# A two-branch transformer block on one core: the products of ones ahead of the work read a bf16 constant, twelve of them instead of ten

## The chip, the core and the metric

The kernel runs on one core of a Trainium2 chip. A core has five engines that run side by side, each with its own instructions in a fixed order: TensorE (PE) for matrix products, VectorE (DVE), ScalarE (ACT) and GpSimd (POOL) for elementwise work and reductions, and SyncE (SP), which here only issues transfers. PE reads from SBUF and writes to PSUM, which has eight banks; DVE and ACT copy results back. Sixteen DMA engines move data between the chip's memory and SBUF, and within SBUF. Engines wait for one another through semaphores.

The metric is the device time of one execution in microseconds (us). Lower is better.

## What is computed

The input x is 2048 tokens of 448 numbers. It is normalised per token, and two branches read the result. Branch A is linear attention with 16 heads of 28 features, where queries and keys go through a learned map and two softmaxes. Branch B is a dense layer to 1792 with the Mish activation, and one back. The output is x plus both.

```
xn = (x - mean) / sqrt(var + eps)
q, k, v = split(xn @ wqkv)                      # 16 heads of 28
phi(t) = concat(softmax(t @ w_phi), softmax(-t @ w_phi))
kv, z = phi(k)^T @ v, sum over tokens of phi(k)
A = (phi(q) @ kv) / (phi(q) . z + 1e-6), heads joined, @ wo
h = xn @ w1 + b1;  B = (h * tanh(softplus(h))) @ w2
out = x + A + B
```

All inputs and the output are bf16.

## The kernel before

**Tiling.** The 2048 tokens are 16 tiles of 128, taken in 8 pairs numbered u = 0 to 7; pair 7 is tiles 14 and 15. For each pair the kernel takes the statistics of its two tiles (`ln_stats`, L458), normalises them (`ln_pair`, L492 on DVE or L487 on POOL) and transposes them. Pairs 3 and 2 are transposed on PE (L500) and copied out of PSUM by ACT and DVE (L505, L507). The other pairs are transposed by a transfer that SP issues (L512). The transposed pair, in `xnT`, then feeds the products for v, k and q (helper `pair_part`, L430).

**Weights.** The map w_phi is folded into the query and key weights on the chip, so that one product gives the mapped keys. For the keys, the raw weights `WkR` are loaded (L278), turned on PE against an identity matrix (`w_tr`, L548), copied to SBUF in the buffer `Eq` (L505 on ACT and, for half of the second part, L507 on DVE), multiplied on PE by a block-diagonal arrangement of w_phi (`w_mm`, L571) and copied out again (`Wpk`, L505 on ACT). For the queries, the load itself transposes (L287), and one DVE copy (L291) fills in the last columns.

**Later stages.** The products of keys and values are summed over all pairs (L638). The first dense layer runs in 28 pieces (L430 again, with Mish on ACT at L689). The attention output per tile (L712 and the DVE lines 727 to 738) is transposed, and the two output products (L813 and L829) meet in PSUM, where DVE adds x (L778) before the store.

**Order.** The text `ORDER` (from L147) lists all steps by name, and each engine gets its instructions in that order. A step's name tells its kind, pair and engine: `st15d` is the statistics of tile 15 on DVE, `xn7d` the normalising of pair 7 on DVE, `xt7m` its transposing transfer, `lx4s` the load of x for tiles 8 to 11 from SP. A class `Program` works out the semaphores: an instruction waits for those that wrote what it reads, and an engine runs strictly in order. An instruction that waits so holds back all that stand behind it on its engine. This is so for SP too, where the loads and the transposing transfers share one queue.

On PE the order in front is: `z10`, `wtk0a`, `wtk1b` (the turning of the key weights in two halves), `xt3b`, `xt2d` (the transposes of pairs 3 and 2), `wmk1a`, `wmk0a` (the folding for the keys), then `v3F` and the other value, key and query products. On DVE it is: statistics of tiles 7, 4 and 5, normalising of pairs 3 and 2, the copies for `wtk1b`, `xt3b` and `xt2d`, statistics of tiles 15, 14 and 13, `xn7d`, and `qd` (L291). On SP, `xt7m` comes after the first loads, and `lx4s` comes behind it.

**The step that is changed.** `z10` calls `warm(10)` (L370 to L378). It takes one PSUM bank and runs ten products of a 128 x 128 block of ones with a 128 x 512 block of ones. Both are one column of a constant read over and over. Nobody reads the result. The step waits for nothing and stands first on PE.

Of the kernel before, what the change touches and what calls it, by code (L numbers as in the profile page):

```python
# [9 lines left out]
BF16 = mybir.dt.bfloat16  # L10
# [6 lines left out]
P = 128  # L17
# [13 lines left out]
def ap_on(src, dims):  # L31
    return bass.AP(tensor=src.tensor, offset=src.offset, ap=[list(src.ap[0])] + [list(d) for d in dims])
# [112 lines left out]


ORDER = """  # L147
lx3s st7d lx2s lks pi pp lpa table st4d st5d pw z10 st6a rs3a pm rs2t xn3d lvts bd wtk0a pv lvms lx6s xn2d wtk1b xt3b
xt2d wmk1a lqT0 st15d lx0s lqT3 lqT1 lqT2 wmk0a st14d v3Fd rs7a st13d xn7d v2Hd v3Ha k3H k2H lx1s pk k2F v2Fa qd wmq1a
st12d st3d st2d k3F wmq0d lbs xt7m v7Fd lx4s k7F l1ts rs1p rs6a xn1d q2H st10d xn6p l1m2s k7H xt1m st1d st11d v7Hd q3H  # L150
xt6m q3F rs5p xn5p st0d st8d q2F e6 v1Fa st9d q1F xt5m k1H v1Hd rs4t q1H e7 k6H xn4d kn2.1 kn2.0 k1F k6F rs0a e2 v5Fd
# [17 lines left out]
def _kernel(es, nc, A_x, A_wqkv, A_w_phi, A_wo, B_w1, B_b1, B_w2, out):  # L169
    def sb(name, shape, dtype):  # L170
        return es.enter_context(nc.sbuf_tensor(name, shape, dtype))
# [4 lines left out]
    ident = sb("ident", [P, P], BF16)  # L176
# [71 lines left out]
    def bank(b, n=1):  # L248
        return PS[:, b * TCW:(b + n) * TCW]
# [10 lines left out]
    def pb(b):  # L260
        return ("ps", b)
# [107 lines left out]

    def warm(n):  # L370
        b = take1()
        one = nc.const_aps.scalar_like(1.0, ident[:, 0:1])

        def f(e):
            for _ in range(n):
                ins = e.matmul(bank(b)[:, :], ap_on(one, [[0, P]]), ap_on(one, [[0, TCW]]), start=True, stop=True)  # L376
            return ins
        pe(f, [], [pb(b)], f"warm{n}")  # L378
# [25 lines left out]
    def take1():  # L404
        b = min((b for b in range(8) if b - b % 2 not in held), key=lambda b: used[b])
        touch(b)
        return b

    def pe(fn, r, w, tag):
        return op("PE", fn, r=r, w=w, tag=tag)  # L410
# [499 lines left out]
    for n in (4, 8, 10, 12, 14):  # L910
        add(f"z{n}", warm, n)
# [53 lines left out]
```

## Time and profile before

| | before |
|---|---|
| time, median of three runs | 162.64 us (162.0 to 162.92) |
| the profiled execution: time | 161.87 us |
| its span, first to last instruction | 160.0 us |
| PE busy | 154.5 us, 97% of the span |
| DVE, ACT, POOL busy | 64%, 45%, 25% |
| products of ones (L376) | 20 records, 0.84 us to 12.18 us |

The page of the profile has numbered parts. Part 1 gives each engine's busy time. Part 2 cuts the span into 40 slices of 4 us and gives the busy share of each in tenths. Part 4 is the chain of work that ended last, followed back from the last instruction. In rows with an engine, the first number is the start and the second the length, both in us from the span's start; xN counts the instructions that a row merges, and a bracket at the end gives the idle time of the engine ahead of it and what ended it. "PEld" is the loading of a product's stationary operand, "SPq" a transfer being issued on SP's queue. The ends of PE's products are modelled by the profiler, and they overlap: their spacing is read from their starts.

### The profile page before, as it was taken

How to read it: one execution, taken by the hardware profiler on the slowest of the kernel's cores; microseconds unless marked ns; L12 is line 12 of the kernel's file. 1: busy time of each engine (PE TensorE's matmuls, PEld its weight loads, DVE VectorE, ACT ScalarE, POOL GpSimd, SP SyncE). 2: the span in 40 equal slices, each digit the busy share in tenths (PEclk: the TensorE clock that was granted, in tenths of full speed). 3: DMA queues.
4: the chain of work that ended last, by engine and by line, in shares of the span. 5: the costliest groups of instructions: out<-in, count | busy, mean ns of one | idle time of the engine just before them, and what ended most of it. 6: DMA issues, size and time to landing. Idle time of an engine off the chain costs nothing.

```text
span 160.0 us, 2916 instructions
## 1 busy us (share of the span) xinstructions
PE 154.5 (97%) x1193; PEld 75.6 (47%) x1193; DVE 101.6 (64%) x225; ACT 71.9 (45%) x94; POOL 39.5 (25%) x55
## 2 busy tenths in 40 slices
PE   7999989999989999999999999999999999999993
PEld 3447443444434346543444444555545555445552
DVE  0906958699959990307574856959979899311241
ACT  3607897899689984353885685500000000000000
POOL 6700026439998999000000000000000000000000
PEclk9999999999999999999999999999999999999999
DMA  5991489899998299599005300050022212510005
GB/s 142 299 193 48 36 212 217 159 166 172 226 198 201 41 190 353 153 185 83 0 4 105 64 12 4 0 104 16 0 57 49 82 46 57 161 44 0 0 0 201
DMA packets 40058, 17.12 MB, mean 107 GB/s; under 512 B 33965, under 2 KB 39277, under 8 KB 40045
## 3 DMA queue, kind: packets, MB, share of 16 engines
q1 hardware_dynamic: 39436, 16.81, 48.8%
q8 instruction: 9, 0.15, 0.4%
q10 hardware_dynamic: 608, 0.12, 0.4%
q14 instruction: 5, 0.03, 0.1%
HBM read 6.97 MB, written 1.84 MB: 55 GB/s over the span
## 4 chain that ended last, share of the span: by engine, by line
PE 79%; DMA 8%; ACT 6%; DVE 2%; SPq 2%; issue 1%; ACTq 0%; DVEq 0%
PE PS L430 33%; PE PS L813 26%; PE PS L376 7%; PE PS L829 7%; DMA EqT<-actT 3%; DMA xnT<-xn 3%; DMA x_all<-in_A_x_dram 3%; PE PS L712 2%; PE PS L638 2%; ACT actT L670 1%; ACT Wpk L505 1%; ACT actT L609 1%; ACT Eq L505 1%; DVE KVT L650 1%; SPq L678 1%
## 5 line engine op out<-in xcount | busy, mean ns | idle before, releaser
L430 PE MATMUL PS<-xnT,W 128*128 128x512 bf16 (+1 forms) x224 | 45.7, 379 | 0.2 <-ACT actT L689 0.2
L813 PE MATMUL PS<-W,actT 128*128 128x448 bf16 (+1 forms) x224 | 43.3, 351 | 0.0
L689 ACT ACTIVATE actT<-PS,b1T 128x1024 bf16<-128x1024 f32 x28 | 30.1, 1113 | 17.5 <-PE PS L430 13.1
L813 PEld LDWEIGHTS PS<-W,actT 128*128 128x128 bf16 x224 | 21.8, 98 | 20.2 <-issue 0.2
L430 PEld LDWEIGHTS PS<-xnT,W 128*128 128x128 bf16 (+1 forms) x224 | 17.5, 97 | 24.2 <-issue 4.1
L621 POOL TENSOR_TENSOR actT<-actT,rSk 128x896 bf16<-128x896 bf16 x16 | 26.6, 1696 | 5.3 <-DVE rSk L619 5.2
L778 DVE TENSOR_TENSOR x_all<-PS,x_all 128x448 bf16<-128x448 f32 (+1 forms) x16 | 9.2, 614 | 15.2 <-PE PS L829 8.0
L617 DVE TENSOR_REDUCE Sk<-actT 128x32 f32<-128x896 bf16 x16 | 16.6, 1039 | 0.0
L727 DVE COPY Sq<-PS 128x16 f32<-128x16 f32 x32 | 4.0, 168 | 17.1 <-PE PS L712 17.1
L609 ACT ACTIVATE actT<-PS 128x896 bf16<-128x896 f32 x16 | 13.8, 939 | 1.7 <-PE PS L430 1.7
L430 PE MATMUL PS<-Wv,xnT 128*128 128x448 bf16 (+1 forms) x64 | 13.0, 352 | 1.0 <-DMA xnT<-xn 0.6
L430 PE MATMUL PS<-Wpk,xnT 128*128 128x448 bf16 (+1 forms) x64 | 12.8, 353 | 0.2 <-DMA xnT<-xn 0.2
L430 PE MATMUL PS<-Wpq,xnT 128*128 128x448 bf16 (+1 forms) x64 | 12.6, 353 | 0.1
L376 PE MATMUL PS<-const-float32-1.0 128*128 128x512 f32 x20 | 11.3, 732 | 0.8 <-PEq L950 0.8
L458 DVE BATCH_NORM_STATS2 stats<-x_all 128x6 f32<-128x448 bf16 x15 | 9.1, 607 | 4.2 <-DMA x_all<-in_A_x_dram 4.1
L735 DVE TENSOR_TENSOR v_all<-v_all 128x464 f32<-128x464 f32 x16 | 10.3, 643 | 0.6
L731 DVE TENSOR_TENSOR v_all<-PS,Sq 128x464 f32<-128x464 f32 x16 | 10.3, 641 | 0.5
L738 DVE TENSOR_TENSOR xn<-v_all,rden 128x448 bf16<-128x448 f32 x16 | 10.0, 625 | 0.6
L733 DVE TENSOR_TENSOR v_all<-PS,Sq 128x464 f32<-128x464 f32 x16 | 10.1, 630 | 0.0
L670 ACT ACTIVATE actT<-PS 128x896 bf16<-128x896 f32 x10 | 8.7, 922 | 2.4 <-PE PS L430 1.7
L430 PEld LDWEIGHTS PS<-Wv,xnT 128*128 128x128 bf16 (+1 forms) x64 | 5.1, 96 | 6.9 <-issue 1.7
L430 PEld LDWEIGHTS PS<-Wpq,xnT 128*128 128x128 bf16 (+1 forms) x64 | 5.1, 97 | 6.2 <-issue 1.4
(85 smaller groups left out, 117.2 us busy)
## 6 DMA issues: line engine op xcount, KB each, us to landing
W<-in_B_w_dram SPq DMA_DIRECT2D x1, 1568.0 KB, 7.7
out_dram<-x_all SPq DMA_DIRECT2D x7, 224.0 KB, 2.2
W<-in_B_w_dram SPq DMA_DIRECT2D x3, 448.0 KB, 4.6
x_all<-in_A_x_dram SPq DMA_DIRECT2D x4, 224.0 KB, 3.2
x_all<-in_A_x_dram SPq DMA_DIRECT2D x2, 448.0 KB, 4.9
Wo<-in_A_wo_dram SPq DMA_DIRECT2D x2, 336.0 KB, 9.0
W<-in_B_w_dram SPq DMA_DIRECT2D x2, 224.0 KB, 4.9
WkR<-in_A_wqkv_dram SPq DMA_DIRECT2D x1, 392.0 KB, 4.7
```

Source lines behind the costliest of these rows:

```text
L376: ins = e.matmul(bank(b)[:, :], ap_on(one, [[0, P]]), ap_on(one, [[0, TCW]]), start=True, stop=True)
L430: ins = e.matmul(o, lhs(c, k), rhs(c, k), start=first and c in (0, 3), stop=not first and c in (2, 3))
L609: op("ACT", lambda e, s=s: e.activation(E_of(u)[:, s, :, :], two(b, D), ACT.Exp, scale=1.0 if s == 0 else -1.0), r=[pb(b), pb(b + 1)], w=[ ...
L617: op("DVE", lambda e: e.tensor_reduce(Sk[u][:, s, :], Eh(), AX.X, ALU.add), r=[("E", u, s)], w=[("Sk", u, s)], tag=f"Sk{u}.{s}")
L621: op("POOL", lambda e: e.tensor_tensor(Eh(), Eh(), ap_on(rSk[u][:, s, 0:1], [[1, 2 * H], [0, DH]]), ALU.mult), r=[("E", u, s), ("rSk", u, ...
L670: op("ACT", lambda e, s=s: e.activation(Eq_of(u)[:, :, s, :].rearrange("p i (h n) -> p i h n", n=64)[:, :, :, 0:QP], two(b, D).rearrange(" ...
L689: op("ACT", lambda e: e.activation(actT[:, fc, q * 1024:(q + 1) * 1024], bank(b, 2), ACT.Mish, bias=b1T[:, fc:fc + 1]), r=[("b1T",), pb(b) ...
L731: op("DVE", lambda e: e.tensor_tensor(tv(t1[i]), num(0), sx(1), ALU.mult), r=[pb(b), pb(b + 1), ("Sq", i, 1)], w=[("t1", i)], tag=f"ta{t}")
L733: op("DVE", lambda e: e.tensor_tensor(tv(t2), num(1), sx(0), ALU.mult), r=[pb(b), pb(b + 1), ("Sq", i, 0)], w=[("t2",)], tag=f"tb{t}")
L735: op("DVE", lambda e: e.tensor_tensor(t1[i], t1[i], t2, ALU.add), r=[("t1", i), ("t2",)], w=[("t1", i)], tag=f"tc{t}")
L813: ins = e.matmul(bank(b)[:, 0:width(t)], actT[:, fc, tok(t)], W2[:, fc, 0:width(t)], start=first and fc == 0, stop=last and fc == FC - 1)
L829: ins = e.matmul(bank(b)[:, 0:n], oT_of(u)[lo:hi, cc * P:(cc + 1) * P], Wo[lo:hi, cc, 0:n], start=first and c in (0, 3), stop=last and c i ...
```

## The change

The step `z10` in the order becomes `z12`, and the constant that the products read becomes the bf16 one in place of the fp32 one. Nothing else differs. Both constants are written by POOL in the preamble of either kernel.

```
 ORDER = """
-lx3s st7d lx2s lks pi pp lpa table st4d st5d pw z10 st6a rs3a pm rs2t xn3d lvts bd wtk0a pv lvms lx6s xn2d wtk1b xt3b
+lx3s st7d lx2s lks pi pp lpa table st4d st5d pw z12 st6a rs3a pm rs2t xn3d lvts bd wtk0a pv lvms lx6s xn2d wtk1b xt3b
...
     def warm(n):
         b = take1()
-        one = nc.const_aps.scalar_like(1.0, ident[:, 0:1])
+        one = nc.const_aps.tensor(1.0, (P, 1), BF16)

         def f(e):
             for _ in range(n):
```

More of the change, by code (lines that the diff above doesn't have):

```diff
@@ L147 @@
 ORDER = """
-lx3s st7d lx2s lks pi pp lpa table st4d st5d pw z10 st6a rs3a pm rs2t xn3d lvts bd wtk0a pv lvms lx6s xn2d wtk1b xt3b
+lx3s st7d lx2s lks pi pp lpa table st4d st5d pw z12 st6a rs3a pm rs2t xn3d lvts bd wtk0a pv lvms lx6s xn2d wtk1b xt3b
 xt2d wmk1a lqT0 st15d lx0s lqT3 lqT1 lqT2 wmk0a st14d v3Fd rs7a st13d xn7d v2Hd v3Ha k3H k2H lx1s pk k2F v2Fa qd wmq1a
@@ L371, in warm @@
         b = take1()
-        one = nc.const_aps.scalar_like(1.0, ident[:, 0:1])
+        one = nc.const_aps.tensor(1.0, (P, 1), BF16)
         def f(e):
```

## The prediction

> **What bounds the kernel now.** I read the page's parts 1 and 2 first. They say which engine is busy, and when.
>
> ```profile
> span 160.0 us, 2916 instructions
> PE 154.5 (97%) x1193; PEld 75.6 (47%) x1193; DVE 101.6 (64%) x225; ACT 71.9 (45%) x94; POOL 39.5 (25%) x55
> PE   7999989999989999999999999999999999999993
> DVE  0906958699959990307574856959979899311241
> ACT  3607897899689984353885685500000000000000
> POOL 6700026439998999000000000000000000000000
> PEclk9999999999999999999999999999999999999999
> DMA  5991489899998299599005300050022212510005
> ```
>
> PE is busy for 97% of the span. But in slice 2 (8 to 12 us) DVE, ACT and POOL all stand still, and in slices 3 and 4 (12 to 20 us) the DMA engines are mostly idle, while PE is "busy". Something that PE does in front holds the others. The chain that ended last, read from its start, names it:
>
> ```profile
> 0.84 11.34 PE PS L376 x20
> 12.18 0.51 PE PS L548 x10
> ...
> 17.43 0.58 DVE xn L492 x2
> ...
> 19.35 4.34 DMA x_all<-in_A_x_dram
> 23.69 4.47 DMA xnT<-xn
> ...
> 28.29 15.69 PE PS L430 x90
> ```
>
> The products of ones (L376) hold PE to 12.18. Only then come the turned key weights (L548), their copy (ACT), the folded weights, the normalised pair 7 (DVE L492), its transposing transfer on SP's queue, and behind that in the same queue the load of x that feeds PE at 28.29. From there the chain is nearly all PE to the end. So 11.3 us of dummy work lie on the path that sets the end.
>
> **What the ones cost, before and after.** The timeline of PE, asked in short windows, gives the spacing. A row has the start, the length from the first start to the last end, and the count.
>
> ```profile
> 1.82 1.06 PE L376 MATMUL PS<-const-float32-1.0 128*128 128x512 f32 x1
> 1.82 1.91 PE L376 MATMUL PS<-const-float32-1.0 128*128 128x512 f32 x2
> 5.98 1.02 PE L376 MATMUL PS<-const-float32-1.0 128*128 128x512 f32 x2
> 12.02 1.17 PE L548 MATMUL PS<-ident,WkR 112*112 112x112 bf16 x20
> 52.62 0.81 PE L430 MATMUL PS<-xnT,W 128*128 128x512 bf16 x3
> 52.62 1.24 PE L430 MATMUL PS<-xnT,W 128*128 128x512 bf16 x5
> ```
>
> Ten fp32 products leave 20 records (the chain's x20), two each. The first starts at 0.84 and the second at 1.82; from there a further record lengthens the row by 1.91 - 1.06 = 0.85 us. If that spacing held, 14 more from 5.98 would end far behind 12.02, where L548 follows. They are spaced (12.02 - 5.98) / 14 = 0.43 us, half of it. So PE runs at half speed until shortly before 5.98 and at full speed after. The PEclk row shows 9 throughout and does not see it, so I read speed from spacing alone. The sum fits: starts at 0.84, then 1.82 and four more at 0.85 make six records up to about 5.98, and 14 x 0.43 lead from there to 12.02.
>
> A bf16 product of 512 columns is one record; two of them take 1.24 - 0.81 = 0.43 us, so 0.215 us each at full speed, half of an fp32 record. At half speed no row shows one. Its ends are 0.215 (no slower than at full speed) and 0.85 (an fp32 record at half speed). I take 0.43: the ratio of two between the record kinds, applied to 0.85. Then twelve take 12 x 0.43 = 5.2 us and PE is free at 0.84 + 5.2 = 6.0, not at 12.02. At the low end it is free at 3.4. At the high end there are again six slow records to 5.98, then six at 0.43: free at 8.6. [...]
>
> Removed are 20 records of 11.2 us, added 12 of 5.2 us. The constant costs nothing new, since POOL already writes a bf16 one in the preamble, ahead of the first product:
>
> ```profile
> 0.38 0.10 POOL L950 MEMSET const-bfloat16-1.0<- 128x1 bf16 x1
> ```
>
> Nothing else is moved: on DVE, ACT, POOL and SP the same instructions stand in the same order, and the ones keep the first PSUM bank.
>
> **What is late next.** L548 needs the raw key weights. The rows of SP's queue and of the landings (last number: us from issue to landing):
>
> ```profile
> 1.72 0.42 SPq L278 DMA_DIRECT2D WkR<-in_A_wqkv_dram  x1
> WkR<-in_A_wqkv_dram SPq DMA_DIRECT2D x1, 392.0 KB, 4.7
> 4.05 0.49 SPq L268 DMA_DIRECT2D x_all<-in_A_x_dram  x1
> x_all<-in_A_x_dram SPq DMA_DIRECT2D x1, 448.0 KB, 5.3
> 6.46 3.72 SPq L287 DMA_TRANSPOSE WqT<-in_A_wqkv_dram  x3
> WqT<-in_A_wqkv_dram SPq DMA_TRANSPOSE x2, 3.6
> 10.85 0.47 SPq L302 DMA_DIRECT2D b_rows<-in_B_b_dram  x1
> 18.04 1.26 SPq L512 DMA_TRANSPOSE xnT<-xn  x1
> ```
>
> WkR lands at 1.72 + 4.7 = 6.4. PE could therefore start L548 at 6.4 to 6.5, which is 5.5 us earlier, with about 0.4 us of idle time ahead. It makes no difference whether the ones end at 3.4 or at 6.0. These loads wait for nothing that PE does, so they land when they did. Now DVE:
>
> ```profile
> 6.18 1.96 DVE L492 TENSOR_SCALAR xn<-x_all,mv,rstd 128x448 bf16<-128x448 bf16 x6
> 13.31 0.69 DVE L507 CAST Eq<-PS 112x512 bf16<-112x512 f32 x1 [5.17 <-PE PS L548]
> 14.78 0.62 DVE L458 BATCH_NORM_STATS2 stats<-x_all 128x6 f32<-128x448 bf16 x1
> 17.93 0.22 DVE L291 COPY WqT<-WqT 128x256 bf16<-128x256 bf16 x1
> ```
>
> DVE is busy with pairs 3 and 2 until 8.14. L548's 20 products (1.17 us) end by 7.7, so DVE's copy starts at 8.14 to 8.2 instead of 13.31: 5.1 us earlier (its wait of 5.17 for L548 is gone). This is the tightest link, and it sets the sum. Shifted by 5.1, the next steps meet their loads just in time. The statistics of tile 15 come at 9.7, and its x (issued at 4.05) lands at 9.35. WqT is copied at 12.8, and its last transfer (issued near 8.9, 3.6 us) lands at 12.5. The transposing transfer of pair 7 comes at 12.9, and SP's queue is free from 11.3; before, it stood there until 18.04. The load of x behind it moves from 19.35 to 14.2, and the chain quoted above follows it as a block. The DMA engines, idle between 13 and 18, are then busy again from 12.9.
>
> Behind 28.3 I cost the change at nothing. The stages show why the shift should last:
>
> ```profile
> 12.00:15.10 3.10, 2.74 (x51) 2.54 (x50) 1.79 (x4) 2.05 (x4) 0.00 (x0) 1.00 0.17 62
> 15.10:28.30 13.20, 12.18 (x86) 5.88 (x83) 10.68 (x31) 11.43 (x19) 3.57 (x7) 1.00 0.71 145
> 28.30:75.00 46.70, 46.11 (x374) 21.52 (x375) 31.50 (x58) 34.09 (x44) 30.39 (x24) 1.00 0.91 181
> 75.00:160.00 85.00, 82.27 (x671) 40.91 (x669) 53.46 (x123) 20.11 (x19) 0.00 (x0) 1.00 0.19 47
> ```
>
> (Columns: length, busy time of PE, PE loads, DVE, ACT, POOL, then clock, DMA share, GB/s.) PE works 46.1 of 46.7 and 82.3 of 85.0 us, on inputs that all hang on the shifted chain. **The sum**: of the 6.0 us that the ones give back, WkR's landing takes 0.4 and DVE's pairs 3 and 2 another 0.5; what is left is the 5.1 us of DVE's copy. The profiled execution took 161.87 us (1.87 outside the span) and would take 156.8. The median of the three runs stands 0.77 above it, so 162.64 - 5.1 = 157.5.
>
> **The rivals.**
>
> *Half speed lasts one stretch longer.* PE needed some 5.0 us of unbroken work to reach full speed (0.84 to shortly before 5.98). The twelve ones last 5.2, then come some 0.4 us without work. If the rise misses this stretch, PE must earn it again from 6.45, to about 11.5. The 20, 14 and 16 small products ahead of the first value product took 15.14 - 12.02 = 3.1 us at full speed with 2.7 busy; doubled they end near 11.7, a shift of 3.4 instead of 5.1. That gives 159.2. If it misses that stretch too, another 5 us at half speed cost 2.5 more, less the idle 1.4 us of the first two stages above: 160.3. For it: there is nearly no margin. Against it: at half speed the small products leave PE hardly idle, and whatever counts PE's work sees a gap of only 0.4. [...] Chance 0.18.
>
> *It is slower: PE stays at half speed through the front.* Place: 6.45 to 24 us, where the work is broken up. Price: a stretch of T us at half speed loses T/2 of work. The gain of 5.1 plus 1.4 us of idle time is used up at T = 13, that is if the rise comes only at about 19 us. At 24 us it costs 17.5/2 - 1.4 = 7.4, so 2.3 more than is won: 164.9. For it: nothing in the trace shows how soon the speed rises when PE's work is broken up, as it is there. Against it: between 12.0 and 28.3 PE is idle for only 1.4 us of 16.3, and at half speed it would be idle for less. Chance 0.08.
>
> *The transfers are the bound and move no earlier.* DMA share is 0.91 from 28.3 to 75. If this stage can't end sooner, the time is 162 to 163. Against it: its first transfer waits for pair 7 alone, and the engines stand idle ahead of it. Chance 0.06, of which 0.05 is within 0.5%.
>
> *A bf16 record costs as much as an fp32 one*, so the change does only half of what it says. PE is free at 8.6, L548's 1.17 us end at 9.8, DVE copies at 10.0, a shift of 3.3: 159.3. The rows at 52.62 speak against it. Chance 0.02.
>
> **How the numbers follow.** The forecast has 0.66, the rivals 0.18, 0.08, 0.06 and 0.02. Half a per cent of this kernel, 0.8 us, is about what a measurement can tell from no change. Faster by more than that: 0.66 + 0.18 + 0.02 + 0.01 = 0.87. Within it 0.05, slower 0.08. The likeliest time is 157.5. Its own range is 156.5 to 158.4: a run 0.9 us to either side, about the spread of the runs shown (162.0 to 162.92). To reach 8 in 10 the range takes in the half-speed case, up to 160.6.
>
> **What would show it.** In the changed profile: 12 bf16 records of L376, spaced 0.43 us, the last ending near 6.2; L548 first at 6.4 to 6.5; DVE's copy (L507) at 8.2 with less than 0.3 us of idle time ahead instead of 5.17; the first transposing transfer of xn at 12.9 instead of 18.04; the 90 products of the chain at 23.2 instead of 28.29; a span near 155. The spacing of the 448-column products in front shows the speed. If it is 0.37 us rather than half of that, the half-speed rivals hold, and the time at which it halves says which. The prediction is wrong if L548 starts early and the transfer of pair 7 does not, or if both are early and the products near 28 us are not.

## The result and the profile after

The changed kernel takes 157.53 us (median of four runs, 157.26 to 157.70), the kernel before 162.32 us (median of four, 161.13 to 162.92). The ratio is 0.971, with a 95% interval of 0.965 to 0.977. On a second chip the same kernel came out at 157.68 us against 161.53, a ratio of 0.976 (0.971 to 0.981). So the change wins 3.7 to 5.6 us on the first chip and 3.0 to 4.6 us on the second. A ratio is taken from the executions within 1.5% of the fastest of their kernel and a median from all of them, so the two can differ a little. The profiled execution of the changed kernel took 157.70 us, 4.2 less than that of before.

The page after has these lines for the span, the engines and the slices:

```profile
span 155.8 us, 2900 instructions
PE 147.9 (95%) x1185; PEld 72.7 (47%) x1185; DVE 101.5 (65%) x225; ACT 71.9 (46%) x94; POOL 39.4 (25%) x55
PE   7799888999989999998999999999999999999993
...
DVE  0998585989679923062757756959969899211241
ACT  3798887997899924709658766200000000000000
...
DMA  5997997999990998690006300330034103610005
```

DVE no longer stands still in slice 2, and the DMA engines no longer in slices 3 and 4. The timelines of PE, DVE and SP's queue show each step of the prediction:

```profile
0.84 4.94 PE L376 MATMUL PS<-const-bfloat16-1.0 128*128 128x512 bf16 x12 [0.84 <-PEq L950]
6.84 1.19 PE L548 MATMUL PS<-ident,WkR 112*112 112x112 bf16 x20 [1.06 <-POOL mask L356]
17.13 1.30 PE L430 MATMUL PS<-Wv,xnT 128*128 128x448 bf16 x6 [0.69 <-DMA xnT<-xn]
23.83 1.29 PE L430 MATMUL PS<-Wv,xnT 128*128 128x448 bf16 x6 [1.03 <-DMA xnT<-xn]
...
8.14 0.69 DVE L507 CAST Eq<-PS 112x512 bf16<-112x512 f32 x1
...
12.87 1.27 SPq L512 DMA_TRANSPOSE xnT<-xn  x1
14.18 1.44 SPq L268 DMA_DIRECT2D x_all<-in_A_x_dram  x1
```

| from the span's start | before | predicted | after |
|---|---|---|---|
| L548 starts | 12.02 | 6.4 to 6.5 | 6.84 |
| DVE's copy for L548 | 13.31 | 8.2 | 8.14 |
| transposing transfer of pair 7 | 18.04 | 12.9 | 12.87 |
| load of x behind it | 19.35 | 14.2 | 14.18 |
| products that waited for xnT | 28.29 | 23.2 | 23.83 |
| sum over keys (L638) starts | 62.38 | 57.3 (62.38 - 5.1) | 57.83 |
| span | 160.0 | near 155 | 155.8 |

The shift is 5.2 us up to the load of x, 4.5 us a little later and 4.2 us at the end. The first difference shows in the waits of PE for the transposing transfers of xn, the second in its wait for ACT's Mish output (L689) at 75.73 us before and 71.53 after. First before, then after:

```profile
PE PS L430 <- DMA xnT<-xn: 0.7, 2, 0.6
PE PS L430 <- ACT actT L689: 0.2, 1, 0.2
```

```profile
PE PS L430 <- DMA xnT<-xn: 1.9, 3, 1.0
PE PS L430 <- ACT actT L689: 0.7, 1, 0.7
```

The waits for xn grew from 0.7 to 1.9 us. A second execution of each kernel (further down) has 1.1 and 1.3 us, so this sum alone says little. Steadier is the one transfer behind the load of x, for which the products at 28.29 and 23.83 us wait. It took 4.47 us before (in the chain at 23.69). After:

```profile
14.18 4.34 DMA x_all<-in_A_x_dram
18.52 5.17 DMA xnT<-xn
```

The second executions say the same, first before, then after:

```profile
22.93 4.54 DMA xnT<-xn
```

```profile
18.43 5.20 DMA xnT<-xn
```

So it lands 0.7 us later in the changed kernel. The stages between 13.5 and 24 us (length, busy time of PE, PE loads, DVE, ACT, POOL, clock, DMA share, GB/s) suggest why. Before:

```profile
13.50:18.00 4.50, 4.14 (x44) 2.25 (x41) 4.34 (x13) 4.08 (x8) 0.00 (x0) 1.00 0.00 0
18.00:24.00 6.00, 5.54 (x42) 3.20 (x41) 4.21 (x14) 5.39 (x9) 0.94 (x2) 1.00 0.88 165
```

After:

```profile
13.50:18.00 4.50, 3.81 (x33) 2.28 (x31) 3.04 (x10) 4.50 (x7) 0.94 (x2) 1.00 0.97 159
18.00:24.00 6.00, 4.97 (x30) 2.12 (x28) 4.79 (x15) 4.73 (x8) 2.77 (x6) 1.00 1.05 222
```

The DMA engines had a pause of at least 4.5 us before. After, they have none there, and PE, no longer the first to hold the front, now waits for them. That the missing pause is what makes the transfer longer is argued from these shares; no run here isolates it.

### The profile page after: what moved, and what is told of

It is laid out like the page before. It is cut to its first block, busy times and chain, and to the rows that moved or that the text cites. A ratio compares the mean times of both kernels' runs of the same rounds, so it can differ in the third digit from the quotient of the medians.

```text
span 155.8 us, 2900 instructions
## 1 busy us (share of the span) xinstructions
PE 147.9 (95%) x1185; PEld 72.7 (47%) x1185; DVE 101.5 (65%) x225; ACT 71.9 (46%) x94; POOL 39.4 (25%) x55
## 3 DMA queue, kind: packets, MB, share of 16 engines
HBM read 6.97 MB, written 1.84 MB: 56 GB/s over the span
## 4 chain that ended last, share of the span: by engine, by line
PE 70%; DMA 14%; ACT 6%; POOL 3%; DVE 2%; SPq 2%; issue 1%; ACTq 0%; DVEq 0%; POOLq 0%
PE PS L430 31%; PE PS L813 27%; PE PS L829 7%; DMA xnT<-xn 6%; DMA EqT<-actT 3%; DMA x_all<-in_A_x_dram 3%; PE PS L712 2%; PE PS L638 2%; DMA Wraw<-in_A_w_phi_dram 2%; POOL xn L487 1%; ACT actT L670 1%; ACT Wpk L505 1%; ACT actT L609 1%; ACT Eq L505 1%; DVE KVT L650 1%
## 5 line engine op out<-in xcount | busy, mean ns | idle before, releaser
L430 PE MATMUL PS<-xnT,W 128*128 128x512 bf16 (+1 forms) x224 | 45.5, 379 | 0.7 <-ACT actT L689 0.7
L689 ACT ACTIVATE actT<-PS,b1T 128x1024 bf16<-128x1024 f32 x28 | 30.2, 1114 | 17.8 <-PE PS L430 12.9
L430 PEld LDWEIGHTS PS<-xnT,W 128*128 128x128 bf16 (+1 forms) x224 | 17.7, 97 | 24.5 <-issue 3.6
L430 PE MATMUL PS<-Wv,xnT 128*128 128x448 bf16 (+1 forms) x64 | 13.0, 352 | 1.9 <-DMA xnT<-xn 1.9
L430 PE MATMUL PS<-Wpk,xnT 128*128 128x448 bf16 (+1 forms) x64 | 12.8, 353 | 0.0
L430 PE MATMUL PS<-Wpq,xnT 128*128 128x448 bf16 (+1 forms) x64 | 12.6, 353 | 0.1
L430 PEld LDWEIGHTS PS<-Wv,xnT 128*128 128x128 bf16 (+1 forms) x64 | 5.1, 96 | 7.9 <-ACT Eq L670 1.4
L430 PEld LDWEIGHTS PS<-Wpq,xnT 128*128 128x128 bf16 (+1 forms) x64 | 5.2, 97 | 6.2 <-issue 1.4
L430 PEld LDWEIGHTS PS<-Wpk,xnT 128*128 128x128 bf16 (+1 forms) x64 | 5.1, 97 | 5.7 <-issue 1.1
```

Of the source, the lines that this page charges most:

```text
L430: ins = e.matmul(o, lhs(c, k), rhs(c, k), start=first and c in (0, 3), stop=not first and c in (2, 3))
L689: op("ACT", lambda e: e.activation(actT[:, fc, q * 1024:(q + 1) * 1024], bank(b, 2), ACT.Mish, bias=b1T[:, fc:fc + 1]), r=[("b1T",), pb(b) ...
```

## The experiments

Four theories are told apart. *A*: only the time at which PE comes free behind the ones counts, and the type of the constant does not. *C*: PE needs its stretch of work for full speed, and the ones supply it. *D*: the moved front runs into the transfers. *E* came up on the way: a stretch without work behind the ones can take the speed away again. All diffs are against the changed kernel.

**Four products in fp32, and forty in bf16.** The first lets L548 start as early as the change does, with the old type; the second as late as the kernel before, with the new type.

```
-pw z12 st6a                      # the order
+pw z4 st6a
...
-        one = nc.const_aps.tensor(1.0, (P, 1), BF16)
+        one = nc.const_aps.scalar_like(1.0, ident[:, 0:1])
```

> Four products of ones in fp32 instead of twelve in bf16. Theory A (only the time at which PE comes free counts): eight records, six spaced 0.85 us and two 0.43 us, end near 6.8 us, where the key weights land anyway; the time stays within 0.6 us of the changed kernel, 157.0 to 158.2 us. Rival B (reading fp32 ones holds the front back as such, or bf16 ones raise the speed of PE sooner): 159 us or more, with the turning of the key weights (L548) at 0.1 us per product instead of 0.05 or starting behind 8 us.

Measured: 159.09 us (158.13 to 160.13), ratio 0.989 (0.983 to 0.995). L548 started at 6.92 at full speed (its 20 products took 1.19 us, as in the changed kernel), the load of x at 14.47, and the products that waited for xnT began at 23.72, as in the changed kernel.

```
-pw z12 st6a
+pw z40 st6a
```

> Forty products of ones in bf16. Theory A: about eleven or twelve at 0.43 us up to 5.3 to 5.9 us and the rest at 0.215 us end at 11.5 to 12.0 us, as late as the ten fp32 ones did; L548 starts there, and the time is that of the kernel before within 0.7 us, 161.6 to 163.0 us. Rival B (the type of the constant is what counts): 157 to 158.5 us.

Measured: 160.38 us (160.05 to 161.30), ratio 0.995 (0.991 to 0.998). The timeline of PE:

```profile
0.84 11.16 PE L376 MATMUL PS<-const-bfloat16-1.0 128*128 128x512 bf16 x40 [0.84 <-PEq L950]
11.84 1.18 PE L548 MATMUL PS<-ident,WkR 112*112 112x112 bf16 x20
```

With bf16 ones that last as long as the fp32 ones, four fifths of the gain are gone: 0.5% is left of the 2.4 to 2.9% that the change wins on two other chips. So theory A has the main cause: the length of the dummy work. But both times miss its ranges, and in the same sense.

The fp32 kernel is 0.9 us above its range. It keeps 1.1%, less than half of the gain, and its time lies where rival B put it, although B's signs (slow or late key weights) are absent from its profile. That profile is of the fastest of its four executions; where the other three lost up to 2 us more is not on record.

The bf16 kernel lies below its range, even if the range is taken from the kernel before on this chip (161.47 - 0.7 us). Its profile and the first one of the kernel before differ by 0.18 us at L548, but by 1.08 us at the products behind xnT (27.21 against 28.29): the transfer in between took at most 3.7 us instead of 4.47. Beside the second profile of the kernel before (further down), whose fp32 ones let L548 start 0.58 us sooner, its span is 0.4 us longer, which leaves nothing for the type. So whether the type costs anything beside its length stays open.

**Twenty-four products in bf16.**

```
-pw z12 st6a
+pw z24 st6a
```

> Twenty-four products of ones in bf16. Theory A: PE comes free at 8.1 to 8.6 us, L548 starts 1.3 to 1.8 us later than in the changed kernel, and every microsecond of that is in the end: 158.8 to 159.5 us. Rival (DVE or the loads have slack behind 8.2 us, so that the first microseconds are free): 157.5 to 158.3 us.

Measured: 158.82 us (157.51 to 159.44), ratio 0.984 (0.977 to 0.991). L548 started at 8.07, and the load of x at 15.40, both 1.2 us later than in the changed kernel. The median is in theory A's range. The profiled execution, the fastest of the four, is not: its products behind xnT began at 24.13, only 0.3 later than in the changed kernel, since PE's waits for xn were 0.8 us instead of 1.9. So part of the front's shift is paid out again at the transfers, which is theory D.

**No products of ones.**

```
-pw z12 st6a
+pw z0 st6a
...
     def warm(n):
         b = take1()
+        if n == 0:
+            return
```

> No products of ones at all, the PSUM bank taken as before. Theory C (PE needs its stretch of work to reach full speed, and the ones supply it): L548 starts at 6.7 to 6.9 us at 0.1 us per product, the first value products are spaced 0.37 us, and full speed comes at 10.5 to 13.5 us; the first value product comes 1.7 to 2 us later than in the changed kernel, and the time is 159.0 to 160.5 us. Rival (the front has slack for half speed): 157.2 to 158.2 us. Rival (PE stays at half speed through the front, to 20 us or more): 162 us or more.

Measured: 159.67 us (158.50 to 160.79), ratio 0.991 (0.986 to 0.995). The rows of PE (two lines were added above, so L550 is the L548 of the other kernels, and L432 is L430):

```profile
6.37 2.05 PE L550 MATMUL PS<-ident,WkR 112*112 112x112 bf16 x20 [6.37 <-DMA WkR<-in_A_wqkv_dram]
8.23 1.68 PE L502 MATMUL PS<-ident,xn 128*128 128x128 bf16 x14
9.70 1.46 PE L573 MATMUL PS<-Wbd,Eq 112*128 112x112 bf16 x16
10.99 1.79 PE L432 MATMUL PS<-Wv,xnT 128*128 128x448 bf16 x10
```

L548's products took 2.05 us instead of 1.19, the 14 transposes behind them 1.68 instead of 0.95, and the first value product came at 10.99 instead of 9.97. The first ten value products took 1.79 us, their length at full speed (1.78 in the changed kernel). The time lies in theory C's range, though the first value product came 1.0 us later and not 1.7 to 2: without the ones the front runs at half speed for some 4 us (from 6.37 to a point between 9.70 and 10.99, by these rows). It also bounds the other side: half speed in front does not last to 20 us, and it leaves a gain of about 1% over the kernel before.

**The changed kernel and the kernel before, once more.**

> The changed kernel once more, beside the others of this set on one chip. Theory A says its ratio to the kernel before stays 0.968 to 0.975 and PE again waits 1.5 to 2.2 us for transposing transfers of xn in front. If these waits belonged to one execution alone, the profile shows 0.7 us as before and a span 1 us shorter.

Measured: 157.68 us (157.07 to 158.81), ratio 0.976 (0.971 to 0.981), just above the range expected. PE waited 1.3 us for xn's transfers, a little under the range expected and well above 0.7; the span is 155.7. For every execution the mean of the clock that was granted to PE is on record. It is 1.000 in five of the six, and 0.989 in the one of 158.81 us, 1.3 us above the median of the others. The runs with the weights moved, below, show what such a value stands for: one stretch at half speed under way. In the runs above, every execution has 0.998 or more.

> The kernel before once more, for a second profile of it. Theory A: the ones end at 11.1 to 12.8 us, since the moment at which PE reaches full speed differs from one execution to the next (twenty records of 0.43 us at full speed, 0.85 us at half), and the span follows that. Theory D: PE waits 0.7 us or less for the transfers of xn, and the DMA share between 13.5 and 18 us is under 0.1.

Measured: one execution of 160.20 us, with a span of 158.4. The ones ended earlier than in the first profile, so L548 started at 11.26, and PE waited 1.1 us for xn's transfers, more than the 0.7 expected; the DMA share from 13.5 to 18 us was 0.00. In this second pair of profiles the shift is 4.4 us at the load of x (18.59 against 14.16), 3.9 at the products behind xnT (27.61 against 23.76) and only 2.7 at the end. Here PE did not wait for L689 before, and waited 0.6 us for it after. The kernel before varies from 159.97 to 163.42 us in the 23 runs beside this set. Between its two profiles L548 moved by 0.76 us and the time by 1.67, so when PE reaches full speed is probably one part of that.

**The dense layer's weights later.** If the transfers of xn land late because loads are in flight beside them, loads that are not needed yet can be moved away.

```
-lx4s k7F l1ts rs1p
+lx4s k7F rs1p
...
-xn6p l1m2s k7H
+xn6p k7H
...
-q6H l1m1s k5H
+q6H l1ts l1m2s l1m1s k5H
```

> The changed kernel with the loads of the first dense layer's weights (672 KB: two tails and the third chunk) issued on SP's queue some 17 us later, ahead of the load of the second chunk. Theory D (the moved front runs into the transfers: the DMA share between 13 and 24 us is 0.9 to 1.0 and the transposing transfers of pairs 7, 1 and 6 land later for it): PE's waits for xn's transfers fall from 1.9 us to 1.0 us or less, and the time is 0.5 to 1.0 us below the changed kernel. Rival (the transposing transfers are slow by themselves): the waits and the time stay within 0.4 us of the changed kernel. Rival (the later loads collide with the transfers of the features, or hold the dense layer): slower by 0.5 us or more.

(Each tail is 224 KB and the chunk 448 KB, so the moved loads are 896 KB and not 672.)

Measured: 161.33 us (159.71 to 162.83), ratio 0.998 (0.993 to 1.002): the gain is gone. The waits and the timeline of PE in the profile say how:

```profile
PE PS L430 <- DMA xnT<-xn: 2.8, 1, 2.8
PE PS L548 <- DMA WkR<-in_A_wqkv_dram: 1.9, 1, 1.9
...
7.24 1.55 PE L548 MATMUL PS<-ident,WkR 112*112 112x112 bf16 x20 [1.88 <-DMA WkR<-in_A_wqkv_dram]
8.60 1.68 PE L500 MATMUL PS<-ident,xn 128*128 128x128 bf16 x14
...
23.55 1.30 PE L430 MATMUL PS<-Wv,xnT 128*128 128x448 bf16 x6
...
43.49 1.29 PE L430 MATMUL PS<-Wpk,xnT 128*128 128x448 bf16 x6 [2.76 <-DMA xnT<-xn]
```

The move did what theory D says where it was aimed. The waits for xn up to 24 us are gone, and the products there began at 23.55, although pair 7 had been 1.3 us later than in the changed kernel. But the moved loads met the transfer of pair 0, and PE stood 2.8 us for it at 41 to 43 us. That is the last rival of the forecast. And in front something else happened: the key weights, which are issued long before the loads that were moved, landed late in this execution, PE stood for 1.88 us, and then it worked at half speed again. This time the clock in the table of stages shows it (length, PE busy, clock, DMA share, GB/s):

```profile
7.00:7.50 0.50, 0.26 (x6) 1.00 1.05 324
7.50:8.00 0.50, 0.50 (x13) 0.86 1.10 393
8.00:9.00 1.00, 1.00 (x13) 0.50 1.24 283
...
11.00:12.00 1.00, 1.00 (x12) 0.86 0.59 115
12.00:13.00 1.00, 1.00 (x8) 1.00 0.52 183
```

This stretch brings the mean clock of the execution to 0.989 (by the shares in these rows it was at half speed from 7.86 to 11.28 us; 3.4 us at half speed in 159 take 0.011 off the mean). All twelve executions of this version lie at 0.979 to 0.989, so each had one such stretch or two, and this is part of the lost gain. At which of the two waits the executions without a profile had it is not on record.

A second version put the load of x for tiles 8 to 11 ahead of pair 7's transfer as well.

```
-lbs xt7m v7Fd lx4s k7F rs1p      # on top of the diff above
+lbs lx4s xt7m v7Fd k7F rs1p
```

> As the one with the late weights, and the load of x for tiles 8 to 11 goes on SP's queue ahead of the transposing transfer of pair 7 instead of behind it, so at 11.3 us instead of 14.2 us. Theory D: the load lands 2.5 to 3 us sooner and DVE no longer waits 0.6 us for it at 18.5, but it collides with the transfer of pair 7, for which PE waits at 17.1; the two about cancel, within 0.6 us of the one with the late weights. Rival (x for tiles 8 to 11 is what the front waits for): faster than it by 1 us or more.

Measured: 161.27 us (160.16 to 162.64), ratio 0.998 (0.995 to 1.002), within 0.1 us of the one above, as theory D expected. Its profile has half speed twice, each time behind a wait of PE, and a mean clock of 0.979. The second is the wait for pair 0:

```profile
6.94 1.74 PE L548 MATMUL PS<-ident,WkR 112*112 112x112 bf16 x20 [1.84 <-DMA WkR<-in_A_wqkv_dram]
...
43.72 1.31 PE L430 MATMUL PS<-Wpk,xnT 128*128 128x448 bf16 x6 [3.03 <-DMA xnT<-xn]
44.95 2.42 PE L430 MATMUL PS<-Wv,xnT 128*128 128x448 bf16 x6
```

Six products that take 1.30 us elsewhere took 2.42 us.

**Sixteen products, and the weights behind pair 0.** Sixteen ones shorten the stretch without work; with them the weights were moved once more, past the transfer that they had met.

```
-pw z12 st6a
+pw z16 st6a
```

> Sixteen products of ones instead of twelve. They end at 6.2 to 6.9 us, about when the key weights land, so the stretch without work ahead of L548 shrinks from 1.1 to 1.9 us to under 0.9 us. Theory E (with a stretch of about 1.9 us PE falls back to half speed, as in the two profiles with the late weights, with 1.4 us it does not): never at half speed behind the ones, the time that of the changed kernel or up to 0.5 us below, ratio to the kernel before 0.970 to 0.978, with a smaller spread. Rival (the ones delay L548): slower than the changed kernel by 0.3 us or more.

Measured: 157.69 us (156.60 to 158.37), ratio 0.980 (0.972 to 0.988). PE stood 0.57 us ahead of L548 and kept its full speed (L548 took 1.19 us, and the clock is 1.00 in every row from 5 to 14 us); the mean clock of all six executions is 0.998 to 1.000. The time is that of twelve; the ratio is just above the range expected, and the spread is no smaller.

```
-lx4s k7F l1ts rs1p               # with z16
+lx4s k7F rs1p
...
-xn6p l1m2s k7H
+xn6p k7H
...
-xt0m e12 e13
+xt0m l1ts l1m2s e12 e13
```

> Sixteen products of ones, and the same loads of the dense layer's weights moved behind the transposing transfer of pair 0 instead of ahead of it. Theory D: PE's waits for xn's transfers up to 24 us fall to 0.7 us or less, as they did with the late weights, and the wait of 2.8 us near 41 us that came there is gone; the time is 0.5 to 1.2 us below that of sixteen products alone. Rival (the transfers take the time wherever the loads stand): within 0.4 us of it. Rival (the loads now hold the dense layer): a wait of PE near 47 us, slower by 0.5 us or more.

Measured: 158.35 us (156.71 to 159.13), ratio 0.982 (0.974 to 0.990). PE's timeline:

```profile
22.18 1.30 PE L430 MATMUL PS<-Wv,xnT 128*128 128x448 bf16 x6
...
47.64 3.07 PE L430 MATMUL PS<-xnT,W 128*128 128x512 bf16 x14 [1.82 <-ACT Eq L670]
51.35 7.94 PE L430 MATMUL PS<-xnT,W 64*128 64x512 bf16 x40 [0.64 <-ACT actT L670]
```

The front came 2 us forward (22.18 instead of 24.23 with sixteen ones alone), with 0.33 us of waits for xn up to there; 0.5 us of that is chance, since the key weights landed sooner in this execution (L548 at 6.76 instead of 7.22). Then, as I read the chain (a transfer of features from 45.17 us took 4.33, and ACT's next exponentials began at 49.57), the loads held the transfers of the features, ACT had no free buffer for its exponentials, and PE stood 1.8 us for them at 46 us. The sum over keys started at 59.29, later than the 58.49 with sixteen ones alone. So up to 24 us most of the waits come from the loads beside the transfers. But the DMA engines have little room behind that (a share of 0.89 from 24 to 70 us in the changed kernel), and moving a load within it moved the wait. No version here beats the change.

**The key weights later, with twelve and with twenty products.** The load of the key weights goes behind two small loads, so that PE stands longer behind twelve ones and, as was meant, not at all behind twenty.

```
-lx3s st7d lx2s lks pi
+lx3s st7d lx2s pi
...
-xn3d lvts bd
+xn3d lvts lks bd
```

> Twelve products of ones, and the load of the raw key weights goes on SP's queue behind the two small loads of the value weights, so 1.2 us later. Theory E: PE stands for 2 to 3 us behind the ones, falls back to half speed, and the time is 2.0 to 3.5 us above the changed kernel, 159.5 to 161.3 us, of which 0.8 to 1.2 us is the later landing and the rest the half speed. Rival (the speed does not fall back in so short a time): only the landing counts, 158.2 to 159 us.

Measured: 158.53 us (157.35 to 159.51), ratio 0.985 (0.974 to 0.996). The four runs are two of 159.4 to 159.5 us with a mean clock of 0.989, the profiled one among them, and two of 157.4 to 157.6 us with 0.999 and 1.000. In the profiled one PE stood 2.38 us, and was then at half speed (a clock of 0.50 from 9 to 11 us):

```profile
7.99 1.80 PE L548 MATMUL PS<-ident,WkR 112*112 112x112 bf16 x20 [2.38 <-DMA WkR<-in_A_wqkv_dram]
9.60 1.68 PE L500 MATMUL PS<-ident,xn 128*128 128x128 bf16 x14
```

> As the one with the late key weights, with twenty products of ones, which end at 7.3 to 7.8 us and leave no stretch without work. Theory E: PE stays at full speed and the time is 1 us or more below that with twelve, 158.0 to 159.2 us. Rival: the same time as with twelve, within 0.4 us.

Measured: 158.41 us (157.94 to 158.70), ratio 0.984 (0.978 to 0.991). PE stood 0.65 us and kept its full speed (L548 took 1.22 us, and the clock is 1.00 from 5 to 14 us), and the mean clock is 1.000 in all four executions. The medians do not differ, so theory E's difference of 1 us failed. But its sign is in the profile, and the clocks say which executions had it: with twelve ones the fall came in two of four, and these are 1.8 to 2.2 us longer than the two without it. With twenty it never came, but the time is 0.9 us above that of the two with twelve that had no fall. Where this 0.9 us went is not shown.

## Why the prediction was right

**The place of the loss.** That the ones held the front, and that DVE, ACT and the DMA engines stood still for them, is shown: forty bf16 ones (L548 at 11.84) left a gain of half a per cent, and four fp32 ones (L548 at 6.92) kept part of it.

**The price of a bf16 product at half speed.** I took 0.43 us between 0.215 and 0.85. The rows of the changed kernel say 0.43: 1.49 - 1.06, where a further record starts.

```profile
1.22 1.06 PE L376 MATMUL PS<-const-bfloat16-1.0 128*128 128x512 bf16 x2
1.22 1.49 PE L376 MATMUL PS<-const-bfloat16-1.0 128*128 128x512 bf16 x3
```

**What is late next.** The key weights landed 5.0 us after their issue in the changed kernel instead of 4.7, and up to 5.6 us in other executions, so PE stood 1.06 us and not 0.4. (The bracket at 6.84 names POOL, but the landing, 1.72 + 5.0 us, is what came just ahead, as in the profiles whose brackets name it.) That cost next to nothing. DVE was free at 8.00 (6.03 + 1.97) and L548 ended at 8.03, so the two links were about equally tight, and the copy came at 8.14; in the second profile L548 came 0.10 us sooner, and pair 7's transfer 0.01. Pair 7's transfer and the load of x behind it came within 0.03 us of the forecast.

**The step that failed: the block that follows the load of x as a whole, and "Behind 28.3 I cost the change at nothing".** The shift was 5.2 us at that load, 4.5 at the products behind xnT and 4.2 at the end of the two first profiles. About 0.7 us was lost before 24 us, to the transfer behind the load, which took 5.17 us instead of 4.47 once the work ahead of it had moved into the pause of the DMA engines. Another 0.3 us was lost behind the sum over keys, where a transposing transfer of actT took 4.98 us instead of 4.63 and PE's wait for L689 grew from 0.2 to 0.7 us. In the second pair of profiles the two losses are 0.6 and 1.0 us, and the shift at the end is 2.7. The rival that named the transfers as the bound, at a chance of 0.06, held in this part. So the term of 5.1 us should have been 2.7 to 4.2 by the profiles. The medians moved by 4.8 on the first chip and by 3.9 on the second, and that the forecast of 157.5 meets 157.53 is in part luck: the median of before came down by 0.3 with its fourth run, and the profile of the changed kernel stands 0.2 above its median, where that of before stood below.

**Half speed for a stretch longer.** The two profiles of the changed kernel do not have it, with 1.06 and 1.42 us without work behind the ones. One of its ten executions, without a profile, has the mean clock that goes with it (0.989, 158.81 us). Three profiles of its variants have it, behind 1.84, 1.88 and 2.38 us. So the rival is real, at a price of some 1.3 to 2.2 us in the few executions that show it, but not as I wrote it: PE had reached full speed by the end of the ones (in the profile with the late weights their last record took 0.38 us, where those at half speed take 0.63, and six products of L548 began in the 0.26 us from 7.24, at a clock of 1.00) and lost it again. The fear that PE stays slow through the front is answered by the kernel without ones, which is still faster than before (159.67 us, a ratio of 0.991).

## What to carry to other kernels

Dummy work that is to bring PE to speed should end about when the first real operand lands: here twelve ones ended at 5.78 us and the key weights landed at 6.7. What it overruns is paid at the end, if the other engines hang on it: forty ones held L548 to 11.84 and left a gain of 0.5% where twelve have 2.4 to 2.9%. A pause between it and the work can take the speed back, as 1.84, 1.88 and 2.38 us did here. Whether it did is in the granted clock of each execution (a mean of 0.989 in the profiles with one such stretch, 0.979 in the one with two, 0.998 or more in those with none), so look there before calling a longer execution noise. When the front of a kernel moves forward, look which pause of which queue it moves into: here the transfers filled one, and 0.7 us of 5.2 was lost at them. Moving a load within a full queue moved the wait here (none for xn up to 24 us, but 2.8 us for pair 0 at 41 to 43), so look where it comes up again before counting the gain.

## What the runs showed of the hardware

PE fell back to half speed after 1.84, 1.88, 2.38 and 3.03 us without work, but not after 1.42 us (ahead of L548 in the second profile of the changed kernel, where L548 took 1.19 us), nor after 1.82 us (the row at 47.64 above, 14 products in 3.07 us), nor after 2.76 us in the profile with the late weights (the row at 43.49, six products in 1.29 us). Whether it falls is thus not a matter of the length alone; what else decides it, no run here shows. Each of these four falls lasted 3.4 us by the clock column (in the profile with the late weights from about 7.86 to 11.28 us, worked out from its shares of 0.86 in two rows above), and set in 0.4 to 1.1 us after PE was back at work.

The row of the granted clock shows such a fall, but not the slow start: it read full speed in every slice of the kernel before while its first products were spaced 0.85 us. The start has to be read from the spacing.
